# A fused attention and gated-MLP kernel: order of loads and sums around the last 512 rows of the gate stage

## The chip, the cores and the metric

The kernel runs on one core of a Trainium2 chip, in one launch. The metric is the device time of a whole execution in microseconds (us), the median of the runs shown. One more execution is recorded by the hardware profiler; it has a time of its own, and the durations below come from it. The engines of the core are PE (TensorE matmuls; PEld are its weight loads), ACT (ScalarE), DVE (VectorE), POOL (GpSimd) and SP (SyncE, which here only issues transfers). Each takes its own instructions strictly in order. The transfers of all queues run on 16 DMA engines.

## The reference

```
xn = layernorm(x)                                  # x: 2048 x 640, bf16
q  = (xn @ wq) as 32 heads of 192                  # wq: 640 x 6144
k, v = the last 512 of 2048 cached rows, 32 heads of 192
s  = concat(softmax(q k^T / sqrt(192)) v) @ wo     # wo: 6144 x 640
h  = sigmoid(xn @ w_gate) * (xn @ w_up)            # 640 x 1536 each
g  = silu(h @ w_down)                              # w_down: 1536 x 640
out = x + s * g
```

## The kernel before, in words

The kernel has a hand-written order: no scheduler moves an instruction. It has three phases.

**Gate stage (the loop at line 475, to about 134 us of the profile).** The 2048 rows are taken in four steps `s` = 0..3 of 512 rows. Each step has twelve blocks `f` of 128 hidden columns. A block is ten matmuls of 128x512 on PE (line 487: five with the gate weights `wg_sb`, five with the up weights `wu_sb`), a sigmoid on ACT (L492) and a product on DVE (L493) that writes `hT_sb`. The two results of a block take one pair of PSUM banks out of four pairs in turn, so block `f+4` can't start before the sigmoid of block `f` has read its first bank, nor its second half before the product of block `f` has read the second.

The rows of step `s+1` are normalized during step `s` (`ln_at`): statistics on DVE, then at block 4 a square root on ACT (L365, with a table load before and after it), then `ln_rest` at blocks 5 and 6: DVE writes the normalized rows `xn` (L372) and SP issues their DMA transpose (L441), two per block. Steps 1 and 3 use the one buffer `x_odd`; steps 0 and 2 use `x_even[0]` and `x_even[1]`, which lie in the tile `mid`.

Into the same loop a hand-made list puts other work, keyed by (step, block):

- `scan_loads`, `scan_act`, `folds`: the weights `wq` are read in 16 pieces to find a magnitude for scaling them. SP loads a piece (L201), ACT sums its absolute values (L300), or DVE folds it into a running maximum `wmax` (L207, L209).
- `abs_at`: ACT sums the absolute values of `w_up` in four parts (L303).
- L523 reduces `wmax`; `set_scale` (L212 to L217) reduces all sums, rounds to a power of two and has SP issue a small DMA transpose `mx_row`; `set_scale2` (L220 to L222) takes the maximum over the partitions and sets `w_up` (the scale by which `wq` is multiplied; a column of `w_sc`) and `w_down` (that of the keys).
- `swap` at the start of steps 1 and 3: four SP transfers (L445 to L448) that exchange halves of the partitions of `x_even` and `x_odd` into `XC` and `x_sw`. `sums` says at which blocks DVE does the six sums `sum_x` of a pair of steps (L455 to L465, 64x2560 each) that read them. The query projection in the next phase is done with such sums (a Strassen-like scheme).
- In step 3: `scale_w` at blocks 0, 2, 5, 8 (ACT, one L244 and two L249) and `sum_w` at blocks 1, 3, 6, 9 (DVE L262, L263, L265, L266, with one ACT copy L249 between) prepare the query weights, and POOL issues the load of the next piece (L230). `scale_k` (DVE L167) at blocks 0 and 7 and `turn_k` (SP DMA transpose L172) at blocks 3 and 9 prepare the first two key tiles; their raw keys come by `load_k` (L158).

The results `hT_sb` of steps 0 to 2 are written to DRAM (`h_d`, L548). Step 3 uses its own at once: four output tiles `q`, each of twelve pairs of matmuls, 128x512 and 128x128 (L557), with the down weights `wd_sb`, then sigmoid and product (L564, L565).

**Attention (lines 763 to 966, about 134 to 660 us).** Sixteen runs of scores (L697), exponentials (L701), values (L711) and query products (L603).

**End (from line 1109).** The output products and the rest of the gate products (L1019), then the output.

SP's queue around the change stands in this order: scan pieces and `h_d` of step 1, three raw pieces of `wq` (L230); in step 2 two transposes of `x_odd`, `mx_row`, two more transposes, `wd_sb` (L528), four `v_sb` (L181), two `kraw` (L158), four `h_d`; in step 3 `swap`, then the key transposes. SP has eight completion semaphores that it uses in turn, so that a transfer is not issued before the eighth one ahead of it has landed.

Of the kernel before, what the change touches and what calls it, by code (L numbers as in the profile page):

```python
# [17 lines left out]
def kernel(  # L18
# [13 lines left out]
    nc = tc.nc  # L32
# [17 lines left out]
    TQ = 4  # L50
# [28 lines left out]
    def bank2():  # L79
        if bank_order:  # L80
            b = bank_order.pop(0)
        else:
            b = ring.pop(0)
            ring.append(b)
        return ps_all[:, 2 * b:2 * b + 2, :]
# [9 lines left out]
    h_d = [dram.tile([P, NF, P], BF16, name=f"h_d{t}") for t in range(NM3 * TQ)]  # L95
# [58 lines left out]
    def load_k(key, eng=nc.sync):  # L154
        kraw = kraw_pool.tile([P, 2, KC * PC, HF], BF16, name="kraw")
        for i in range(2):
            hk = (2 * (key[0] * G + key[1]) + i) // rep
            eng.dma_start(  # L158
                kraw[:, i, :, :],
                A_k_cache[0, hk, Sk - W:Sk, :].rearrange("(p k) (j e) -> p (k j) e", k=KC, e=HF),  # L160
            )
        kraw_of[key] = kraw
# [56 lines left out]
    def set_scale2(mx=mx, up=w_up, down=w_down, k=1.0 / 4096):  # L219
        nc.vector.tensor_reduce(mx, mx_row[:, 0, :], axis=mybir.AxisListType.X, op=ALU.max)  # L220
        nc.vector.tensor_scalar(down, mx, k, None, op0=ALU.mult)
        nc.vector.reciprocal(up, down)  # L222
# [3 lines left out]
    def load_raw(g, c, eng):  # L226
        raw = raws[raw_next[0] % 3]
        raw_next[0] += 1
        for r in (LO, HI):
            eng.dma_start(raw[r], wq_r[:, c, :, g * GC:(g + 1) * GC])  # L230
        raw_t[g, c] = raw
# [43 lines left out]
    with ExitStack() as bctx:  # L275
# [167 lines left out]
        def swap(pi):  # L443
            x_sw = xt_pool.tile([P, 2, NCD, 512], BF16, name="x_sw")
            nc.sync.dma_start(XC[pi][LO], x_odd[HI])  # L445
            nc.sync.dma_start(XC[pi][HI], x_odd[HI])
            nc.sync.dma_start(x_sw[HI, 0], x_even[pi][LO])
            nc.sync.dma_start(x_sw[HI, 1], x_odd[LO])  # L448
            return x_sw

        def sum_x(pi, k, x_sw):
# [12 lines left out]
            elif k == 5:  # L464
                tt(xb[HI], ev[HI], xb[HI], ALU.subtract)  # L465

        sums = {(1, 4): (0, 4), (1, 10): (0, 0), (1, 11): (0, 1), (2, 7): (0, 2), (2, 8): (0, 3), (2, 10): (0, 5),
                (3, 4): (1, 0), (3, 5): (1, 1), (3, 8): (1, 2)}
        folds = {(1, 7): 9, (1, 8): 10, (1, 9): 11}
        scan_act = {(0, 7): 0, (0, 8): 1, (0, 9): 2, (0, 10): 3, (1, 1): 4, (1, 2): 5, (1, 3): 6, (1, 5): 7, (1, 6): 8,  # L470
                    (2, 0): 12, (2, 1): 13, (2, 2): 14, (2, 3): 15}
        scan_loads = {(0, 8): (4, 5, 6), (0, 9): (7,), (0, 10): (8,), (0, 11): (9,), (1, 1): (10, 11), (1, 7): (12, 13, 14, 15)}
        abs_at = [(0, 3), (0, 4), (2, 6), (2, 8)]
        ln_at = {0: (2, (1, 1, 2), 5), 1: (0, (1, 1, 1, 1), 4), 2: (0, (1, 1, 1, 1), 4)}
        for s in range(NST):
            hT_sb = hpool.tile([P, TQ, NF, P], BF16, name="hT_sb")
            pi = s // 2
            if s % 2 == 1:
                sw = swap(pi)
            for f in range(NF):  # L480
                if s == 0 and f < FA:
                    gu = gu_first[f]
                else:
                    gu = bank2()
                    for i, w in enumerate((wg_sb, wu_sb)):
                        for c in range(NCD):
                            nc.tensor.matmul(  # L487
                                gu[:, i, :], lhsT=w[:, c, f * P:(f + 1) * P], rhs=xnT[s][:, c, :],
                                start=(c == 0), stop=(c == NCD - 1),
                            )  # L490
                sig_sb = bwork.tile([P, 512], BF16, name="sig_sb")
                nc.scalar.activation(sig_sb[:], gu[:, 0, :], AF.Sigmoid)  # L492
                nc.vector.tensor_tensor(  # L493
                    hT_sb[:, :, f, :], *(v.rearrange("p (q n) -> p q n", q=TQ) for v in (gu[:, 1, :], sig_sb[:])),
                    ALU.mult,
                )
                if s + 1 < NST:
                    t = (s + 1) * TQ
                    f0, counts, f1 = ln_at[s]
                    n = f - f0  # L500
                    if 0 <= n < len(counts):
                        for q in range(sum(counts[:n]), sum(counts[:n + 1])):
                            ln_stats(t + q)
                    if f == f1:
                        ln_rstd(t, t + TQ)
                    n = f - f1 - (1 if s else 0)
                    if 0 <= n < 2:
                        ln_rest(t + 2 * n)
                        ln_rest(t + 2 * n + 1)
                if (s, f) in sums:  # L510
                    sum_x(*sums[s, f], sw)
                if (s, f) in folds:
                    scan_fold(wmax, folds[s, f], folds[s, f] == 9)
                if (s, f) in scan_act:
                    scan_abs(scan_act[s, f], 1 + list(scan_act).index((s, f)))
                if (s, f) in abs_at:
                    abs_up(abs_at.index((s, f)))
                if (s, f) in ((0, 8), (1, 7)):
                    load_x4(s + 2)
                for i in scan_loads.get((s, f), ()):  # L520
                    scan_load(i, nc.sync)
                if s == 2 and f == 4:
                    nc.vector.tensor_reduce(  # L523
                        scans[:, 0:1], wmax[:].rearrange("p c n -> p (c n)"), axis=mybir.AxisListType.X, op=ALU.max)
                elif s == 2 and f == 5:
                    set_scale(scans[:])
                elif s == 2 and f == 8:
                    nc.sync.dma_start(wd_sb[:], B_w_down.rearrange("(f p) d -> p f d", p=P))  # L528
                    for hp in range(G):
                        load_v(0, hp, nc.sync)  # L530
                    load_k((0, 0), nc.sync)
                elif s == 2 and f == 9:
                    set_scale2()
                if s == 3:
                    for c in {0: (0,), 2: (1,), 5: (2,), 8: (3,)}.get(f, ()):
                        scale_w(0, c)
                    for c in {1: (0,), 3: (1,), 6: (2,), 9: (3,)}.get(f, ()):
                        sum_w(0, c)
                        load_raw((c + 3) // NCD, (c + 3) % NCD, nc.gpsimd)
                    if f in (0, 7):  # L540
                        scale_k((0, f // 7))
                    elif f in (3, 9):
                        turn_k((0, f // 9))
                    if f == 0:
                        load_k((0, 1), nc.gpsimd)
            if s < NM3:
                for q in range(TQ):
                    nc.sync.dma_start(h_d[s * TQ + q][:], hT_sb[:, q, :, :])  # L548
                if s == 1:
                    for c in range(3):  # L550
                        load_raw(0, c, nc.sync)
                continue
            for q in range(TQ):
                oB_ps = flat(bank2())
                for f in range(NF):
                    for d0, dsz in d_chunks:
                        nc.tensor.matmul(  # L557
                            oB_ps[:, d0:d0 + dsz], lhsT=hT_sb[:, q, f, :],
                            rhs=wd_sb[:, f, d0:d0 + dsz],
                            start=(f == 0), stop=(f == NF - 1),  # L560
                        )
                gB_sb = gpool.tile([P, D], BF16, name="gB_sb")
                sg = bone.tile([P, D], F32, name="sg")
                nc.scalar.activation(sg[:], oB_ps[:, 0:D], AF.Sigmoid)  # L564
                nc.vector.tensor_tensor(gB_sb[:], oB_ps[:, 0:D], sg[:], ALU.mult)  # L565
                if q == 0:
                    scale_w(0, NCD - 1)
                elif q < 3:
                    scale_raw(1, q - 1)
                if q == 1:  # L570
                    sum_w(0, NCD - 1)
                    load_raw(1, 2, nc.gpsimd)
                if q < 3:
                    sum_x(pi, 3 + q, sw)
                else:
                    load_k((1, 0), nc.gpsimd)
                t = s * TQ + q
                nc.gpsimd.dma_start(gB_d[t * P:(t + 1) * P, :], gB_sb[:])
# [633 lines left out]
```

## Time and profile before

| | us |
|---|---|
| median of 3 runs | 881.51 (880.75 to 882.6) |
| the profiled execution: its own time | 882.16 |
| its span | 880.3 |
| PE busy | 866.7 (98%) |
| DVE busy | 674.6 (77%) |
| ACT busy | 625.5 (71%) |
| POOL busy | 212.1 (24%) |
| granted PE clock | 1.00 of full speed |

In the rows of the profile, an arrow points from what is read to what is written, `x5` counts instructions that were merged, and a bracket at the end of a timeline row is the time for which the engine was idle before it and what ended that. Ends of matmuls are modelled and reach about 0.16 us into the next row, so intervals are taken from start to start.

### The profile page before, as it was taken

To read this page: it belongs to the slowest core of one execution; us is meant where nothing else is said; L and a number is where in the kernel's file an instruction comes from. 1 tells how busy PE (TensorE), PEld (TensorE's weight loads), DVE (VectorE), ACT (ScalarE), POOL (GpSimd) and SP (SyncE) were. 2 spreads that over 40 slices of the span, in tenths; PEclk is the share of its full clock that TensorE was granted. 3 is DMA by queue.
4 is the path that set the end of the run, shared out by engine and by line. 5 is a ranking of instruction groups with operands and counts; after the bars stand their busy time and mean duration, and the time that the engine had idled before them with its cause. 6 is when DMAs were issued, how large, how long until landed. Compare 5 with 4: busy or idle time off the path is not lost.

```text
span 880.3 us, 18970 instructions
## 1 busy us (share of the span) xinstructions
PE 866.7 (98%) x7558; PEld 567.4 (64%) x7569; DVE 674.6 (77%) x1137; ACT 625.5 (71%) x772; POOL 212.1 (24%) x299
## 2 busy tenths in 40 slices
PE   9999989999999999999999999999999999999998
PEld 5444445757657757757757757757677777777776
DVE  6587477777777777777777777787978687989997
ACT  6858566578978978878878788684655667666662
POOL 0000118607227227217317316300000111000000
PEclk9999999999999999999999999999999999999999
DMA  9998953298698798699798789598688798565851
GB/s 268 267 273 198 306 102 96 73 235 149 179 253 146 179 257 144 186 242 162 174 229 144 185 182 165 145 290 215 179 223 225 227 299 266 161 222 207 277 168 38
DMA packets 264712, 174.69 MB, mean 198 GB/s; under 512 B 162256, under 2 KB 249680, under 8 KB 264624
## 3 DMA queue, kind: packets, MB, share of 16 engines
q1 hardware_dynamic: 258192, 153.23, 67.7%
q0 software_dynamic: 6432, 20.26, 11.5%
q8 instruction: 59, 0.97, 0.5%
q14 instruction: 29, 0.24, 0.1%
HBM read 102.11 MB, written 35.13 MB: 156 GB/s over the span
## 4 chain that ended last, share of the span: by engine, by line
PE 88%; ACT 4%; DVE 2%; DMA 2%; issue 2%; SPq 2%; ACTq 0%; DVEq 0%
PE ps_all L1019 24%; PE ps_all L603 20%; PE ps_all L711 20%; PE ps_all L697 19%; PE ps_all L487 2%; ACT mid L300 1%; DMA x_sw<-x_odd 1%; PE ps_all L557 1%; ACT sig_sb L492 1%; DVE hT_sb L493 1%; SPq L181 1%; DMA mid<-in_A_wq_dram 1%; PE ps_all L395 1%; DMA x_sb<-in_A_x_dram 0%; ACT L492 0%
## 5 line engine op out<-in xcount | busy, mean ns | idle before, releaser
L701 ACT ACTIVATE E<-ps_all 128x1024 bf16<-128x1024 f32 x256 | 251.1, 1022 | 113.5 <-PE ps_all L697 112.9
L697 PE MATMUL ps_all<-qT,kT 64*128 64x512 bf16 x1536 | 198.1, 376 | 0.0
L711 PEld LDWEIGHTS <-E 128*128 128x128 bf16 x2048 | 169.7, 98 | 8.1 <-issue 8.1
L711 PE MATMUL ps_all<-v_sb,E 128*128 128x193 bf16 x2048 | 174.0, 247 | 0.0
L641 DVE TENSOR_TENSOR qT<-ps_all,qp 128x512 bf16<-128x512 f32 x174 | 115.5, 687 | 48.4 <-PE ps_all L603 36.8
L1019 PEld LDWEIGHTS <-mid 128*128 128x128 f16 x1176 | 115.0, 98 | 44.6
L697 PEld LDWEIGHTS <-kT 64*128 64x128 bf16 x1536 | 85.0, 94 | 79.4 <-issue 4.4
L624 DVE COPY qp<-ps_all 128x512 f32<-128x512 f32 x150 | 100.5, 686 | 45.7 <-PE ps_all L603 45.7
L718 DVE TENSOR_TENSOR o_st<-ps_all,rden 128x768 bf16<-128x768 f32 x128 | 122.5, 957 | 4.4
L603 PE MATMUL ps_all<-mid 64*128 64x512 f16 (+1 forms) x840 | 106.2, 376 | 0.4 <-DVE qT L641 0.4
L603 PE MATMUL ps_all<-mid,arm 64*128 64x512 f16 (+1 forms) x840 | 105.6, 376 | 0.0
L603 PEld LDWEIGHTS <-mid 64*128 64x128 f16 x840 | 49.1, 94 | 43.7 <-issue 1.4
L603 PEld LDWEIGHTS <-arm 64*128 64x128 f16 x840 | 47.1, 94 | 44.5
L1019 PE MATMUL ps_all<-arm,mid 128*128 128x320 f16 x462 | 67.5, 299 | 0.0
L832 ACT ACTIVATE mid<-mid,w_sc 128x1536 f16<-128x1536 bf16 (+1 forms) x41 | 60.2, 1493 | 0.5 <-DMA mid<-oT_d 0.5
L244 ACT ACTIVATE mid<-mid,w_sc 128x1536 f16<-128x1536 bf16 x37 | 58.2, 1572 | 0.6
L1019 PE MATMUL ps_all<-op,mid 128*128 128x320 f16 x378 | 55.1, 299 | 0.0
L493 DVE TENSOR_TENSOR hT_sb<-ps_all,sig_sb 128x512 bf16<-128x512 f32 x48 | 32.7, 685 | 25.0 <-ACT sig_sb L492 15.9
L230 POOL DMA_DIRECT2D mid<-in_A_wq_dram x74 | 43.9, 598 | 21.8 <-DVE mid L266 21.8
L1019 PE MATMUL ps_all<-mid 128*128 128x320 f16 x336 | 48.2, 299 | 0.0
L262 POOL TENSOR_TENSOR arm<-mid 128x384 f16<-128x384 f16 x20 | 18.1, 904 | 114.7 <-ACT mid L244 113.6
L717 DVE RECIPROCAL rden<-ps_all 128x4 f32<-128x4 f32 x128 | 23.3, 182 | 28.4 <-PE ps_all L711 27.0
(185 smaller groups left out, 1058.0 us busy)
## 6 DMA issues: line engine op xcount, KB each, us to landing
oT_d<-oT SPq DMA_DIRECT2D x64, 384.0 KB, 5.6
mid<-oT_d SPq DMA_DIRECT2D x46, 384.0 KB, 4.7
mid<-in_A_wq_dram POOLq DMA_DIRECT2D x74, 192.0 KB, 6.3
mid<-in_A_wq_dram SPq DMA_DIRECT2D x16, 480.0 KB, 7.7
arm<-in_A_wo_dram SPq DMA_DIRECT2D x16, 480.0 KB, 5.4
v_sb<-in_A_v_cache_dram SPq DMA_DIRECT2D x32, 192.0 KB, 6.0
kraw<-in_A_k_cache_dram SPq DMA_DIRECT2D x28, 192.0 KB, 3.7
h_d<-hT_sb SPq DMA_DIRECT2D x12, 384.0 KB, 7.0
```

The source lines that it names most:

```text
L230: eng.dma_start(raw[r], wq_r[:, c, :, g * GC:(g + 1) * GC])
L244: nc.scalar.activation(raw.bitcast(F16), raw, AF.Copy, scale=w_up)
L493: nc.vector.tensor_tensor(hT_sb[:, :, f, :], *(v.rearrange("p (q n) -> p q n", q=TQ) for v in (gu[:, 1, :], sig_sb[:])), ALU.mult,)
L603: nc.tensor.matmul(ps_all[:, b, :], lhsT=w(r, c), rhs=x[r, c, :], start=(first and k == 0), stop=(k == len(cs) - 1), skip_group_check=True,)
L624: nc.vector.tensor_copy(dst, part(b))
L641: nc.vector.tensor_tensor(q_out(i, u, pp), part(b), t, ALU.add)
L697: nc.tensor.matmul(ps[:, b, :], lhsT=kT[h, c * PC + j, :], rhs=qT_t[r][i, j][h, pp, :], start=(j == 0), stop=(j == PC - 1),)
L701: nc.scalar.activation(E_t[r, i, pp][:, c, :, :], ps, AF.Exp, scale=scale_qk)
L711: nc.tensor.matmul(o_ps[:, q // 2, q % 2, 0:DH + 1], lhsT=E[:, c, h, q * P:(q + 1) * P], rhs=vt[:, c, 0:DH + 1], start=(c == 0), stop=(c = ...
L718: nc.vector.tensor_tensor(o_st[:, :, h * DH:(h + 1) * DH].rearrange("p (b i) d -> p b i d", b=2), o_ps[:, :, :, 0:DH], rden[:].to_broadcas ...
L832: eng.activation(t, t.bitcast(BF16), AF.Copy, scale=up)
L1019: nc.tensor.matmul(ps_all[:, b, d0:d1], lhsT=a[:, c, :], rhs=w[:, c, d0:d1], start=(start and c == 0), stop=(c == nk - 1), skip_group_chec ...
```

## The change

All of it lies in the gate stage. The list of work is the same, instruction for instruction; its order on DVE, ACT and SP differs.

- The loads of the first keys (`load_k((0, 0))`) go from step 2, block 8, behind the down weights and values, to the end of step 1, behind the raw `wq` pieces.
- `wd_sb` goes from step 2, block 8, to step 3, block 1. The values go to step 3, block 5.
- The `h_d` stores of step 2 go from the end of step 2 to step 3, block 1, ahead of `wd_sb`. So `swap` is what SP issues first in step 3.
- The reduction of `wmax` and `set_scale` go from step 2, blocks 4 and 5, to block 8; `set_scale2` from block 9 to block 11. So `mx_row` stands behind all four transposes of `x_odd`.
- Scan pieces 14 and 15: ACT takes them at step 2, blocks 5 and 7, behind the square root, in place of blocks 2 and 3 ahead of it; they are loaded two blocks later, and pieces 7 and 8, whose buffers they take, are summed one block later in step 1. The last two parts of `w_up` go from blocks 6 and 8 to 9 and 10.
- Of the sums, one goes a block back in step 2 (8 to 9), and three in step 3 from blocks 4, 5, 8 to 2, 4, 7.

```diff
-        sums = {(1, 4): (0, 4), (1, 10): (0, 0), (1, 11): (0, 1), (2, 7): (0, 2), (2, 8): (0, 3), (2, 10): (0, 5),
-                (3, 4): (1, 0), (3, 5): (1, 1), (3, 8): (1, 2)}
+        sums = {(1, 4): (0, 4), (1, 10): (0, 0), (1, 11): (0, 1), (2, 7): (0, 2), (2, 9): (0, 3), (2, 10): (0, 5),
+                (3, 2): (1, 0), (3, 4): (1, 1), (3, 7): (1, 2)}
         folds = {(1, 7): 9, (1, 8): 10, (1, 9): 11}
-        scan_act = {(0, 7): 0, (0, 8): 1, (0, 9): 2, (0, 10): 3, (1, 1): 4, (1, 2): 5, (1, 3): 6, (1, 5): 7, (1, 6): 8,
-                    (2, 0): 12, (2, 1): 13, (2, 2): 14, (2, 3): 15}
-        scan_loads = {(0, 8): (4, 5, 6), (0, 9): (7,), (0, 10): (8,), (0, 11): (9,), (1, 1): (10, 11), (1, 7): (12, 13, 14, 15)}
-        abs_at = [(0, 3), (0, 4), (2, 6), (2, 8)]
+        scan_act = {(0, 7): 0, (0, 8): 1, (0, 9): 2, (0, 10): 3, (1, 1): 4, (1, 2): 5, (1, 3): 6, (1, 6): 7, (1, 7): 8,
+                    (2, 0): 12, (2, 1): 13, (2, 5): 14, (2, 7): 15}
+        scan_loads = {(0, 8): (4, 5, 6), (0, 9): (7,), (0, 10): (8,), (0, 11): (9,), (1, 1): (10, 11), (1, 7): (12, 13), (1, 9): (14, 15)}
+        abs_at = [(0, 3), (0, 4), (2, 9), (2, 10)]
...
-                if s == 2 and f == 4:
+                if s == 2 and f == 8:
                     nc.vector.tensor_reduce(
                         scans[:, 0:1], wmax[:].rearrange("p c n -> p (c n)"), axis=mybir.AxisListType.X, op=ALU.max)
-                elif s == 2 and f == 5:
                     set_scale(scans[:])
-                elif s == 2 and f == 8:
+                elif s == 2 and f == 11:
+                    set_scale2()
+                elif s == 3 and f == 1:
+                    for q in range(TQ):
+                        nc.sync.dma_start(h_d[2 * TQ + q][:], h_last[:, q, :, :])
                     nc.sync.dma_start(wd_sb[:], B_w_down.rearrange("(f p) d -> p f d", p=P))
+                elif s == 3 and f == 5:
                     for hp in range(G):
                         load_v(0, hp, nc.sync)
-                    load_k((0, 0), nc.sync)
-                elif s == 2 and f == 9:
-                    set_scale2()
...
             if s < NM3:
-                for q in range(TQ):
+                h_last = hT_sb
+                for q in range(TQ) if s < 2 else ():
                     nc.sync.dma_start(h_d[s * TQ + q][:], hT_sb[:, q, :, :])
                 if s == 1:
                     for c in range(3):
                         load_raw(0, c, nc.sync)
+                    load_k((0, 0), nc.sync)
                 continue
```

## The prediction

> **What bounds the kernel now.** I read the page first, then the windows by stage, then PE's waits.
>
> ```profile
> span 880.3 us, 18970 instructions
> 75.00:100.00 25.00, 23.75 (x110) 10.69 (x110) 15.75 (x28) 13.49 (x19) 0.17 (x1) 1.00 0.83 203
> 100.00:124.00 24.00, 18.33 (x88) 8.04 (x89) 17.10 (x32) 15.57 (x23) 5.78 (x10) 1.00 0.91 194
> 200.00:660.00 460.00, 460.00 (x4642) 311.21 (x4640) 350.11 (x596) 359.87 (x426) 154.53 (x204) 1.00 0.86 192
> ```
>
> After the window come its length and the busy time of PE, PEld, DVE, ACT, POOL, then the granted clock and the share and rate of the DMA engines. From 200 to 660 us PE never stops: this stretch has one length, and whatever is won or lost ahead of it moves the whole rest. Between 100 and 124 us PE is busy for 18.33 of 24 us. That is step 3 of the gate stage, which the change reorders. The clock is 1.00 throughout, so only idle time can be won.
>
> ```profile
> PE ps_all L487 <- ACT sig_sb L492: 2.4, 4, 1.0
> PE ps_all L557 <- DVE hT_sb L493: 2.2, 2, 2.1
> PE ps_all L487 <- issue: 1.1, 1, 1.1
> PE ps_all L487 <- DVE hT_sb L493: 0.9, 1, 0.9
> ```
>
> These four rows of PE's waits (total, times, longest) sum to 6.6 us. They leave out the 0.16 us by which modelled ends reach into a gap, so I measure the loss from start to start, on PE's timeline:
>
> ```profile
> 61.06 1.24 PE L487 MATMUL ps_all<-mid,wg_sb 128*128 128x512 bf16 x5 [0.23 <-DMA mid<-xn]
> ...
> 85.88 1.24 PE L487 MATMUL ps_all<-mid,wu_sb 128*128 128x512 bf16 x5
> 88.26 1.24 PE L487 MATMUL ps_all<-x_odd,wg_sb 128*128 128x512 bf16 x5 [1.14 <-issue]
> ...
> 102.00 1.24 PE L487 MATMUL ps_all<-x_odd,wg_sb 128*128 128x512 bf16 x5 [0.59 <-ACT sig_sb L492]
> ...
> 118.36 2.88 PE L557 MATMUL ps_all<-wd_sb,hT_sb 128*128 128x512 bf16 x19
> 123.29 0.45 PE L557 MATMUL ps_all<-wd_sb,hT_sb 128*128 128x512 bf16 x2 [2.05 <-DVE hT_sb L493]
> 123.89 10.22 PE L557 MATMUL ps_all<-wd_sb,hT_sb 128*128 128x512 bf16 x73 [0.15 <-DVE hT_sb L493]
> 134.05 4.84 PE L603 MATMUL ps_all<-mid 64*128 64x512 bf16 x41
> ```
>
> Step 2 runs without a gap: from its first half-block (61.06) to its last (85.88) are 23 half-blocks, 24.82 / 23 = 1.079 us each, 2.158 a block. It ends at 86.96, and three losses follow:
> - Step 3 starts at 88.26: **1.30 us** lost, waiting for `x_odd`.
> - Step 3 takes 118.36 - 88.26 = 30.10 us for 12 x 2.158 = 25.90: **4.20 us** lost.
> - L557 takes 134.05 - 118.36 = 15.69 us. The last 37 of its 48 pairs, which don't stop, take 134.05 - 123.89 = 10.16, 0.275 each, so 48 need 13.18: **2.51 us** lost, waiting for the products of blocks 10 and 11.
>
> Together 8.01 us. That is all that this change can win there.
>
> **Why they are lost.** SP's, DVE's and ACT's timelines show it:
>
> ```profile
> 79.38 2.56 SPq L441 DMA_TRANSPOSE x_odd<-xn  x2
> 82.04 2.13 SPq L217 DMA_TRANSPOSE mx_row<-mx_b  x1
> 84.26 2.55 SPq L441 DMA_TRANSPOSE x_odd<-xn  x2
> ...
> 101.71 1.45 SPq L448 DMA_DIRECT2D x_sw<-x_odd  x1
> ```
> ```profile
> 76.24 2.12 DVE L523 TENSOR_REDUCE scans<-wmax 128x1 f32<-128x1920 bf16 x1
> ...
> 80.16 0.23 DVE L216 CAST mx_b<-w_sc 128x128 bf16<-128x128 f32 x1
> ...
> 80.90 0.79 DVE L372 TENSOR_SCALAR xn<-x_sb,mv,rstd 128x640 bf16<-128x640 bf16 x2
> ...
> 86.45 0.27 DVE L220 TENSOR_REDUCE w_sc<-mx_row 128x1 f32<-128x128 bf16 x1
> ...
> 86.94 0.16 DVE L222 RECIPROCAL w_sc<-w_sc 128x1 f32<-128x1 f32 x1
> ...
> 98.63 0.90 DVE L167 TENSOR_SCALAR k_sb<-kraw,w_sc 128x768 bf16<-128x768 bf16 x2 [7.26 <-DMA kraw<-in_A_k_cache_dram]
> ...
> 112.11 1.49 DVE L457 TENSOR_TENSOR mid<-x_odd,x_sw 64x2560 f16<-64x2560 bf16 x1 [1.57 <-DMA x_sw<-x_odd]
> ...
> 122.55 1.29 DVE L493 TENSOR_TENSOR hT_sb<-ps_all,sig_sb 128x512 bf16<-128x512 f32 x2 [0.42 <-ACT sig_sb L492]
> ```
>
> The last two transposes of `x_odd` stand behind `mx_row` on SP; their issue ends at 86.81 and PE starts 1.45 later. Then DVE stands still for 7.26 us, because `scale_k` (block 0) waits for keys that SP issued last, behind the down weights and the values. Everything behind it on DVE, and on ACT through the copy in `sum_w`, is late from then on: PE stops from 102.00 on for banks, and again in L557. At 112.11 DVE waits once more, for `x_sw`, whose swap SP issued behind all that.
>
> **Part 1, `x_odd`: 1.30 us.** With `mx_row` moved behind, the four transposes follow each other. Even if `xn` comes no earlier than now (80.90 + 0.79 = 81.69), two issues of 1.28 end at 84.25, and with 1.45 on top `x_odd` is there at 85.7, ahead of 86.96. The square root now has two scan pieces of ACT ahead of it in place of four, so it is more likely earlier; the margin of 1.3 us doesn't need it. The key loads are put ahead of these transposes on SP, but issue in step 1's tail. If they slow a transpose, the bound is these 1.30 us back. I take 0 left.
>
> **Part 2, the scale.** The reduction goes to block 8. PE ends this block at 61.06 + 9 x 2.158 = 80.48; its product is done on DVE by about 81.6, the reduction (2.12) at 83.7, four small operations of at most 0.23 at 84.5. SP issues `mx_row` then, with nothing ahead of it.
>
> ```profile
> wd_sb<-in_B_w_down_dram SPq DMA_DIRECT2D x1, 1920.0 KB, 8.3
> ...
> x_sw<-x_odd SPq DMA_DIRECT2D x1, 320.0 KB, 10.4
> ...
> mx_row<-mx_b SPq DMA_TRANSPOSE x1, 3.5
> ```
>
> The last column is us from issue to landing: 3.5 gives 88.0. Meanwhile DVE has three products (two take 1.29 in the last row above, so 0.65 each) and two sums (1.49) to do, 4.9 us, until 89.4, so `set_scale2` doesn't wait: it takes 0.65 (86.45 to 87.10 in the rows) and ends at 90.1. This is a new wait, with step 3's products and `scale_k` behind it on DVE, and ACT's first `scale_w` behind them. The landing lies between 3.5 and, as for the worst queued transfer, 10.4: at 10.4 the scale would come at 95.6. I take 3.5, the same transfer on a queue as empty.
>
> **Part 3, step 3: 4.20 us, and L557: 2.51 us.** With the keys loaded a step earlier, DVE's 7.26 us are gone. The swap is issued from 84.5 + 2.13 = 86.6 on; at most 1.45 each, its last is issued by 91.0 and even at 10.4 lands at 101.4; the sum that reads it stands at block 4, which DVE reaches at about 102. What is next late is the chain between ACT and DVE itself. Its pieces, where nothing else held them, are these rows of ACT:
>
> ```profile
> 90.03 1.57 ACT L244 ACTIVATE mid<-mid,w_sc 128x1536 f16<-128x1536 bf16 x1
> ...
> 92.72 0.60 ACT L492 ACTIVATE sig_sb<-ps_all 128x512 bf16<-128x512 f32 x1
> ...
> 101.36 0.60 ACT L492 ACTIVATE sig_sb<-ps_all 128x512 bf16<-128x512 f32 x1
> ...
> 104.68 0.60 ACT L492 ACTIVATE sig_sb<-ps_all 128x512 bf16<-128x512 f32 x1
> ...
> 107.23 1.08 ACT L492 ACTIVATE sig_sb<-ps_all 128x512 bf16<-128x512 f32 x2
> ...
> 111.04 0.60 ACT L492 ACTIVATE sig_sb<-ps_all 128x512 bf16<-128x512 f32 x1
> ...
> 115.56 1.08 ACT L492 ACTIVATE sig_sb<-ps_all 128x512 bf16<-128x512 f32 x2
> ...
> 119.36 0.60 ACT L492 ACTIVATE sig_sb<-ps_all 128x512 bf16<-128x512 f32 x1
> ```
>
> The sigmoids named are those of blocks 1, 2, 3, 4 (with 5), 6, 7 (with 8) and 9. From `scale_w`'s L244 to the sigmoid of block 1: 2.69. Block 1 to 2 (through `sum_w`, as from 3 to 4): 107.23 - 104.68 = 2.55. 2 to 3: 3.32. 3 to 6: 6.36. 6 to 7: 2.55 again. 7 to 9: 3.80. 9 to the end of the last product: 122.55 + 1.29 - 119.36 = 4.48. So from 90.1: 92.8, 95.3, 98.7, 105.0, 107.6, 111.4, and 115.9 for the last product. Now PE, from 86.96 without a stop: a block's first half may start when the sigmoid four blocks before is done. Block 7 starts at 102.07 (sigmoid 3 done by 99.3), block 10 at 108.54 (sigmoid 6 done by 105.6): no stop, with more than 2.7 us in hand. The sums in blocks 2, 4 and 7 (1.49 each) and `scale_k` in block 7 lie on DVE while ACT does a `scale_w` (2.7). L557 starts at 86.96 + 25.90 = 112.86 and wants block 11 after eleven pairs, at 112.86 + 11 x 0.275 = 115.88. The chain has it at 115.9. So this wait shrinks from 2.2 us to about 0.1, with nothing in hand: each us by which the scale or the chain is later costs a us there.
>
> **Part 4, what goes behind.** The four `h_d` stores wait for the product of the last block of step 2 (89.4), then `wd_sb` is issued: by 92.4 for the swap and at most 1.45 for each store, 98.2. At 8.3 it lands at 106.5, 6.4 ahead of L557. The first L557 waits for the whole of it. [...] The values and key transposes are wanted in the attention phase, more than 20 us on, and `h_d` hundreds of us on. Scan pieces 14 and 15 add no work to ACT, only move it, behind a square root that is now early. These edits cost 0, covered by PE's matmuls of steps 2 and 3; uncovered, a late `wd_sb` costs its lateness.
>
> **Sum.** 1.30 + 4.20 + (2.51 - 0.1) = 7.9 us. The profiled execution took 882.16, 0.65 above the median of 881.51; it becomes 874.3, the median 873.6.
>
> **Rivals.**
> - *The chain is later than its pieces say* (0.20). `mx_row` lands late, or sums meet the chain, and part of L557's wait stays. For it: nothing in hand at 115.9, and a new wait at `set_scale2`. Against it: the queue ahead of `mx_row` is empty. Price: 1 to 5.4 us of the 7.9 (5.4 with the landing at 10.4): 874.6 to 879.0.
> - *It doesn't do what it says* (0.03). PE's stops only move: ACT and DVE carry so much in step 3 that without the waits they set the pace. They are busy for 15.57 and 17.10 of 24 us even where they waited, so this needs another 6 us of chain: 880 to 882.
> - *Slower* (0.05): the down weights come late. They stand behind the swap, four stores and, on the DMA engines, POOL's key and weight loads. It decides from where `wd_sb` lands after 112.86 + 7.9 = 120.8, which is 22.6 us after issue at 98.2, against 8.3 in the row; landing at 125 gives 873.6 + 12.1 = 885.7. [...] Were the weights to take the swap's 10.4, they would still land at 108.6.
>
> **How the numbers follow.** The forecast has the rest, 0.72, with 873.0 to 874.6 for itself. With most of the first rival the range is 872.9 to 877.0. This kernel's measurements can tell about 0.2% (1.8 us) from no change. Faster by more are the forecast and nearly all of the first rival: 0.92. Within it, the second: 0.03. Slower: 0.05.
>
> **What would show it.** In the profile after, step 3's first matmul should follow step 2's at 1.08 us, no wait of PE on `sig_sb` should stand in step 3, `scale_k` should wait for nothing, and L603 should start near 126.1 in place of 134.05. A wait of L557 for `hT_sb` above 1 us would show the first rival, a wait for `wd_sb` the last. Should L603 start early and the span not shrink, the reading that the rest only shifts is wrong.

## The result and the profile after

The changed kernel takes 873.95 us (median of 6 runs, 873.36 to 874.75) against 882.07 before (6 runs, 880.75 to 883.52); the ratio is 0.9908, with a 95% interval of 0.9895 to 0.9921. The forecast was 873.6. The profiled execution took 874.75 with a span of 873.0. Behind the change its line numbers are three higher than before: L557 is now L560, L603 is L606, L711 is L714.

PE's timeline of the changed kernel, the rows that answer to those of before:

```profile
60.80 1.24 PE L487 MATMUL ps_all<-mid,wg_sb 128*128 128x512 bf16 x5
...
85.62 1.24 PE L487 MATMUL ps_all<-mid,wu_sb 128*128 128x512 bf16 x5
86.70 1.24 PE L487 MATMUL ps_all<-x_odd,wg_sb 128*128 128x512 bf16 x5
...
111.52 1.24 PE L487 MATMUL ps_all<-x_odd,wu_sb 128*128 128x512 bf16 x5
112.60 13.28 PE L560 MATMUL ps_all<-wd_sb,hT_sb 128*128 128x512 bf16 x94
125.82 4.84 PE L606 MATMUL ps_all<-mid 64*128 64x512 bf16 x41
```

No row has a bracket any more: step 3 follows step 2 at 1.08 us, takes 25.90 us and hands over to L560, which runs through in 13.22. From the start of step 2 to the query products it is 125.82 - 60.80 = 65.02 us, where before it was 134.05 - 61.06 = 72.99: 7.97 us are gone. The reason stands in SP's and DVE's timelines. Before, these transfers stood ahead of the swap:

```profile
86.86 0.57 SPq L528 DMA_DIRECT2D wd_sb<-in_B_w_down_dram  x1
87.49 6.16 SPq L181 DMA_DIRECT2D v_sb<-in_A_v_cache_dram  x4
93.70 1.80 SPq L158 DMA_DIRECT2D kraw<-in_A_k_cache_dram  x2
95.60 2.49 SPq L548 DMA_DIRECT2D h_d<-hT_sb  x4
98.13 0.91 SPq L445 DMA_DIRECT2D mid<-x_odd  x1
```

Behind the change, SP and DVE show:

```profile
76.10 5.22 SPq L441 DMA_TRANSPOSE x_odd<-xn  x4
84.17 1.14 SPq L217 DMA_TRANSPOSE mx_row<-mx_b  x1
85.49 0.53 SPq L445 DMA_DIRECT2D mid<-x_odd  x1
...
87.68 1.59 SPq L448 DMA_DIRECT2D x_sw<-x_odd  x1
89.31 5.62 SPq L530 DMA_DIRECT2D h_d<-hT_sb  x4
94.98 1.46 SPq L531 DMA_DIRECT2D wd_sb<-in_B_w_down_dram  x1
96.53 12.38 SPq L172 DMA_TRANSPOSE kT<-k_sb  x1
108.96 2.74 SPq L181 DMA_DIRECT2D v_sb<-in_A_v_cache_dram  x4
```
```profile
90.45 0.74 DVE L167 TENSOR_SCALAR k_sb<-kraw,w_sc 128x768 bf16<-128x768 bf16 x2
...
102.32 1.49 DVE L457 TENSOR_TENSOR mid<-x_odd,x_sw 64x2560 f16<-64x2560 bf16 x1
...
114.31 1.29 DVE L493 TENSOR_TENSOR hT_sb<-ps_all,sig_sb 128x512 bf16<-128x512 f32 x2 [0.42 <-ACT sig_sb L492]
```

The four transposes follow each other, the swap is issued 12.6 us earlier than before (L445 at 85.49 for 98.13), and neither `scale_k` nor the sum that reads `x_sw` has a wait in a bracket. The last transfer of the swap lands 17.8 us earlier (87.68 + 6.6 = 94.3 for 112.1); 14.0 of them are its earlier issue (87.68 for 101.71), 3.8 the transfer itself. What stands behind the down weights on SP now stands there long: the key transpose for 12.38 us.

Of the 7.97 us the span shows 7.3. PE's waits name most of the rest, and two rows of the DMA issues (KB each, us from issue to landing) show how soon the swap landed and what came close:

```profile
PE ps_all L714 <- DVE qT L644: 0.7, 1, 0.7
PE ps_all L606 <- DVE qT L644: 0.4, 1, 0.4
```
```profile
x_sw<-x_odd SPq DMA_DIRECT2D x1, 320.0 KB, 6.6
wd_sb<-in_B_w_down_dram SPq DMA_DIRECT2D x1, 1920.0 KB, 15.6
```

The 0.7 us lie at 227 us in the attention phase, where DVE waited for a key load; a second profile of this kernel (below) does not have them. The 0.4 us were there before. And the down weights landed at 94.98 + 15.6 = 110.6, only 2.0 us ahead of L560.

### The profile page after: what moved, and what is told of

Its sections match the earlier page's. It is cut to its first block, busy times and chain, and to the rows that moved or that the text cites. A ratio compares the mean times of both kernels' runs of the same rounds, so it can differ in the third digit from the quotient of the medians.

```text
span 873.0 us, 18973 instructions
## 1 busy us (share of the span) xinstructions
PE 865.2 (99%) x7558; PEld 567.2 (65%) x7569; DVE 674.6 (77%) x1137; ACT 625.4 (72%) x772; POOL 212.1 (24%) x299
## 4 chain that ended last, share of the span: by engine, by line
PE 95%; ACT 1%; DMA 1%; DVE 1%; SPq 1%; issue 0%; ACTq 0%; DVEq 0%
PE ps_all L1022 24%; PE ps_all L714 20%; PE ps_all L606 19%; PE ps_all L700 18%; PE ps_all L487 11%; PE ps_all L560 1%; DMA kraw<-in_A_k_cache_dram 1%; ACT E L704 1%; PE ps_all L395 1%; DMA x_sb<-in_A_x_dram 1%; ACT arm L759 0%; SPq L158 0%; DVE arm L1006 0%; DVE arm L1077 0%; SPq L330 0%
## 5 line engine op out<-in xcount | busy, mean ns | idle before, releaser
L714 PEld LDWEIGHTS <-E 128*128 128x128 bf16 x2048 | 169.7, 98 | 8.9 <-issue 8.9
L714 PE MATMUL ps_all<-v_sb,E 128*128 128x193 bf16 x2048 | 174.1, 247 | 0.7 <-DVE qT L644 0.7
L606 PE MATMUL ps_all<-mid 64*128 64x512 f16 (+1 forms) x840 | 106.2, 376 | 0.4 <-DVE qT L644 0.4
L606 PE MATMUL ps_all<-mid,arm 64*128 64x512 f16 (+1 forms) x840 | 105.6, 376 | 0.0
L606 PEld LDWEIGHTS <-mid 64*128 64x128 f16 x840 | 49.0, 94 | 43.8 <-issue 1.8
L606 PEld LDWEIGHTS <-arm 64*128 64x128 f16 x840 | 47.1, 94 | 44.6 <-issue 0.2
```

The source lines that it names most:

```text
L606: nc.tensor.matmul(ps_all[:, b, :], lhsT=w(r, c), rhs=x[r, c, :], start=(first and k == 0), stop=(k == len(cs) - 1), skip_group_check=True,)
L714: nc.tensor.matmul(o_ps[:, q // 2, q % 2, 0:DH + 1], lhsT=E[:, c, h, q * P:(q + 1) * P], rhs=vt[:, c, 0:DH + 1], start=(c == 0), stop=(c = ...
```

## The experiments

The question was which part of the change carried the 8 us, and how much was left in hand where the prediction said nothing, or much. Each run's ratio is to the kernel before on the same chip.

**1. The first keys alone.** The kernel before, with the key load at the end of step 1:

```diff
@@ step 2, block 8 @@
-                    load_k((0, 0), nc.sync)
@@ end of step 1 @@
                     for c in range(3):
                         load_raw(0, c, nc.sync)
+                    load_k((0, 0), nc.sync)
```

> The kernel before with one edit of the change: the first keys are loaded at the end of step 1. Theory: DVE's stop of 7.26 us for the keys goes, but the next late thing is the swap, which SP still issues behind down weights, values and stores; without the two key loads ahead of it, it is issued only 1.9 us earlier, so x_sw lands at about 110.2 us in place of 112.1, DVE waits there for some 6 us, and L603 starts 1.9 us earlier. So the kernel gains 1.9 us of the 8.1: a time near 880.2, ratio 0.998. Rival (the losses add up, each with its own cause): the stop for the keys carried the lateness of step 3 and L557, 4.2 + 2.5 us, so the gain is 5 to 6.7 us, a time of 875 to 877, ratio 0.992 to 0.994.

Measured: 880.7 us, ratio 0.9986 (0.9976 to 0.9995). DVE's waits, PE's timeline and PE's windows (length, busy PE, PEld, DVE, ACT, POOL, granted clock, DMA share, GB/s):

```profile
DVE mid L455 <- DMA mid<-x_odd: 3.3, 1, 3.3
DVE mid L457 <- DMA x_sw<-x_odd: 3.0, 1, 3.0
```
```profile
120.74 0.45 PE L557 MATMUL ps_all<-wd_sb,hT_sb 128*128 128x512 bf16 x2 [2.06 <-DVE hT_sb L493]
121.33 11.90 PE L557 MATMUL ps_all<-wd_sb,hT_sb 128*128 128x512 bf16 x74 [0.15 <-DVE hT_sb L493]
133.17 1.04 PE L603 MATMUL ps_all<-mid 64*128 64x512 bf16 x8
```
```profile
118.00:121.00 3.00, 0.94 (x8) 0.34 (x6) 2.47 (x7) 1.60 (x3) 1.18 (x2) 1.00 0.40 89
121.00:124.00 3.00, 2.85 (x13) 1.30 (x12) 1.69 (x3) 2.16 (x2) 0.33 (x1) 0.63 0.51 131
```

The 7.26 us for keys are gone, and in their place DVE waits 6.3 us for the swap, as the theory had it; the rival falls. The gain is smaller than its 1.9 us, and the windows show why: after 3 us in which PE was busy for only 0.94, with the stop of 2.06 us in them, the clock granted in the next 3 us was 0.63. The 37 pairs from 121.33 on took 11.84 us in place of 10.16, so 1.7 us of the gain went with the clock.

**2. The change without its swap order.** The changed kernel, with `wd_sb` and the values issued at step 2, block 8, behind `set_scale`, and the stores at the end of step 2:

```diff
                     set_scale(scans[:])
+                    nc.sync.dma_start(wd_sb[:], B_w_down.rearrange("(f p) d -> p f d", p=P))
+                    for hp in range(G):
+                        load_v(0, hp, nc.sync)
...
-                for q in range(TQ) if s < 2 else ():
+                for q in range(TQ):
```

> The changed kernel, but with the down weights, the values and the step-2 stores of h_d where they were, ahead of the swap on SP; keys, scale and sums as changed. Theory: the swap is issued from about 94.7 us on, XC lands near 101 and x_sw near 108.7, the sums at blocks 2 and 4 wait for them on DVE, and the chain to the last product of step 3 ends near 121 in place of 115.6: 5.4 us of the 8.1 are lost again, a time near 879.4, ratio to before 0.997. Rival (the keys were what counted): as the changed kernel, 874, ratio 0.991.

Measured: 880.37 us, ratio 0.9984 (0.9975 to 0.9993), 6.4 us above the changed kernel: most of the 8.1 us are lost again. DVE's waits, PE's timeline and its window:

```profile
DVE mid L455 <- DMA mid<-x_odd: 8.4, 1, 8.4
```
```profile
106.81 2.29 PE L487 MATMUL ps_all<-x_odd,wu_sb 128*128 128x512 bf16 x5 [4.07 <-DVE hT_sb L493]
108.90 1.52 PE L487 MATMUL ps_all<-x_odd,wg_sb 128*128 128x512 bf16 x5
110.26 1.24 PE L487 MATMUL ps_all<-x_odd,wu_sb 128*128 128x512 bf16 x5
```
```profile
106.00:109.00 3.00, 2.19 (x6) 0.79 (x6) 2.47 (x7) 1.52 (x3) 0.64 (x2) 0.51 1.12 178
```

DVE waits 8.4 us at block 2 for `XC`. The theory's 5.4 us are exceeded by 1.0. The clock can account for that: after the stop of 4.07 us it was 0.51, and the ten matmuls from 106.81 to 110.26 took 3.45 us for 2.16, 1.3 us more.

**3. The change without the later scale.** Scan pieces, reduction, `set_scale` and `set_scale2` at their old blocks (and with them the last parts of `w_up` and the sum that went from block 8 to 9 in step 2):

```diff
-                    (2, 0): 12, (2, 1): 13, (2, 5): 14, (2, 7): 15}
+                    (2, 0): 12, (2, 1): 13, (2, 2): 14, (2, 3): 15}
...
-                if s == 2 and f == 8:
+                if s == 2 and f == 4:
                     nc.vector.tensor_reduce(
...
+                elif s == 2 and f == 5:
                     set_scale(scans[:])
-                elif s == 2 and f == 11:
+                elif s == 2 and f == 9:
                     set_scale2()
```

> The changed kernel, but with the scan pieces, the reduction, set_scale and set_scale2 at the blocks they had before, so that mx_row stands between the transposes of x_odd again; keys, swap and sums as changed. Theory: PE waits 1.3 us for x_odd at the start of step 3 and nowhere else, since the chain of ACT and DVE starts at the same time (L244 near 90) and has 1.3 us more in hand: 1.3 us lost, a time near 875.3, ratio 0.9925. Rival (the chain sets the end of step 3 anyway, PE's earlier start is eaten by it): as the changed kernel, 874, ratio 0.991.

Measured: 874.33 us, ratio 0.9915 (0.9899 to 0.9932). PE's timeline:

```profile
86.83 1.24 PE L487 MATMUL ps_all<-x_odd,wg_sb 128*128 128x512 bf16 x5 [0.39 <-DMA x_odd<-xn]
```

The wait for `x_odd` is back, in the place the theory named and nowhere else, but it is 0.39 us (0.56 from start to start), not 1.14. From the start of step 2 (60.37) to the query products (125.86) it takes 65.49 us, 0.47 more than the changed kernel. The time alone can't tell the two readings apart; the profile shows a wait, of less than half of the size.

**4. The scale 2.1 us later.** A second reduction of `wmax` ahead of `set_scale2`:

```diff
                 elif s == 2 and f == 11:
+                    nc.vector.tensor_reduce(
+                        scans[:, 0:1], wmax[:].rearrange("p c n -> p (c n)"), axis=mybir.AxisListType.X, op=ALU.max)
                     set_scale2()
```

> The changed kernel with the reduction of wmax (2.13 us on DVE) done a second time right ahead of set_scale2, so that w_up is set about 2.1 us later. Theory: the chain had nothing in hand (last product of step 3 done at 115.60 where PE wants it at 115.6), so L557 waits for it by 2.1 us: a time near 876.1, ratio 0.993. Rival (the chain takes up delays, since ACT and DVE stand idle for some us in step 3): 0 to 0.5 us, a time of 874 to 874.5, ratio 0.991.

Measured: 875.67 us, ratio 0.9941 (0.992 to 0.9961), 1.7 us above the changed kernel; one of its five runs took 879.98, at a mean clock of 0.998. PE's timeline:

```profile
116.77 0.45 PE L562 MATMUL ps_all<-wd_sb,hT_sb 128*128 128x512 bf16 x2 [1.06 <-DVE hT_sb L493]
```

L562 (L560 of the changed kernel) starts at 112.28 and takes 15.24 us, to 127.52, for 13.22: the 2.1 us come out as 2.0 in the place predicted. The chain of ACT and DVE in step 3 has nothing in hand, though both stand idle for some microseconds in it.

**5. The swap first, alone.** The kernel before with the sums at blocks 2, 4, 7 and only this moved; keys stay at step 2, block 8:

```diff
-                    nc.sync.dma_start(wd_sb[:], B_w_down.rearrange("(f p) d -> p f d", p=P))
-                    for hp in range(G):
-                        load_v(0, hp, nc.sync)
                     load_k((0, 0), nc.sync)
...
+                elif s == 3 and f == 1:
+                    for q in range(TQ):
+                        nc.sync.dma_start(h_d[2 * TQ + q][:], h_last[:, q, :, :])
+                    nc.sync.dma_start(wd_sb[:], B_w_down.rearrange("(f p) d -> p f d", p=P))
+                elif s == 3 and f == 5:
+                    for hp in range(G):
+                        load_v(0, hp, nc.sync)
```

> The kernel before with one part of the change: stores, down weights and values go behind the swap (and the three sums of step 3 to the earlier blocks). The first keys stay at step 2, block 8, where they now stand alone; scale and scan pieces as before. Theory: the order of the swap against the down weights and values is what carries the gain, and the keys are on time wherever nothing large is ahead of them (issued near 85 us, landing near 90, wanted at 89.8). Left is the wait for x_odd, 0.5 us as in the run with the early scale: a time of 874.3 to 875.3, ratio 0.992. Rival (each part has its own share, the keys' early load among them): 1.2 us or more lost to the early load's absence, 876 or later, ratio 0.9935 or above.

Measured: 874.44 us, ratio 0.9919 (0.9905 to 0.9932), against 881.89 before: 7.4 us of gain from one part (stores, down weights and values together). PE's timeline has one gap left in step 3, at the first block, as long as the waits for `x_odd` though the profile names no releaser for it ("issue"):

```profile
87.16 1.24 PE L487 MATMUL ps_all<-x_odd,wg_sb 128*128 128x512 bf16 x5 [0.49 <-issue]
```

So the early load of the keys is not needed. With the down weights and values gone from ahead of them, the keys land 2.6 us after issue from where they always were:

```profile
kraw<-in_A_k_cache_dram SPq DMA_DIRECT2D x2, 192.0 KB, 2.6
```

**6. The sums at their old blocks** (4, 5, 8) in the changed kernel:

```diff
-                (3, 2): (1, 0), (3, 4): (1, 1), (3, 7): (1, 2)}
+                (3, 4): (1, 0), (3, 5): (1, 1), (3, 8): (1, 2)}
```

> The changed kernel with the three sums of step 3 at blocks 4, 5 and 8 as before. Theory: with the swap on time the sums' place matters only through DVE's queue; two sums in neighbouring blocks push the product of block 6 back by 0.6 us and the chain's end by about 0.5, which L557 waits for: a time near 874.5, ratio 0.9915. Rival (the earlier sums are needed for the gain): 2 us or more lost, 876 or later.

Measured: 873.92 us, ratio 0.9913 (0.9899 to 0.9926). PE's timeline:

```profile
115.16 0.45 PE L560 MATMUL ps_all<-wd_sb,hT_sb 128*128 128x512 bf16 x2 [0.22 <-DVE hT_sb L493]
115.76 10.22 PE L560 MATMUL ps_all<-wd_sb,hT_sb 128*128 128x512 bf16 x74 [0.15 <-DVE hT_sb L493]
```

L560 takes 125.92 - 112.07 = 13.85 us for 13.22, 0.6 more, as expected; the time doesn't show it, since single executions scatter by more (those of the changed kernel from 873.36 to 874.75). The rival falls.

**7. The first key transpose later**, at block 9 instead of 3:

```diff
-                    elif f in (3, 9):
-                        turn_k((0, f // 9))
+                    if f == 9:
+                        turn_k((0, 0))
+                        turn_k((0, 1))
```

> The changed kernel with the first key transpose issued at block 9 of step 3 beside the second, in place of block 3. In the profile of the changed kernel the down weights land 15.6 us after issue, at 110.6, 2.0 us ahead of L557, and SP needs 12.4 us for that transpose. Theory: transpose and weights slow each other on the DMA engines, so the weights land near 104 and SP's transposes take 2 to 5 us each; the time stays near 874, since neither is on PE's path. Rival (stores, keys and query weights ahead of the down weights make them late): they land at 109 to 111 as before, same time.

Measured: 873.49 us, ratio 0.9907 (0.9894 to 0.9921). DMA issues and SP's timeline:

```profile
wd_sb<-in_B_w_down_dram SPq DMA_DIRECT2D x1, 1920.0 KB, 16.3
```
```profile
95.72 13.10 SPq L181 DMA_DIRECT2D v_sb<-in_A_v_cache_dram  x4
```

The theory fell: the weights land 16.3 us after issue, at 110.6 as before, and now it is the values that stand on SP for 13.1 us. So the transpose alone doesn't make the weights late. Whether something that stands right behind them does is not shown, since the values took its place there.

**8. The down weights behind the values**, the prediction's slower case made real:

```diff
                 elif s == 3 and f == 1:
...
-                    nc.sync.dma_start(wd_sb[:], B_w_down.rearrange("(f p) d -> p f d", p=P))
                 elif s == 3 and f == 5:
                     for hp in range(G):
                         load_v(0, hp, nc.sync)
+                    nc.sync.dma_start(wd_sb[:], B_w_down.rearrange("(f p) d -> p f d", p=P))
```

> The changed kernel with the down weights issued at step 3, block 5, behind the first key transpose and the four values, in place of block 1. In the profile of the changed kernel they land at 110.6, 2.0 us ahead of L557 (112.6). Theory (the last rival of the prediction, a mechanism with its price): the DMA engines are busy from 86 to 112 us, so what goes ahead adds its own time: values (0.79 MB) and the key transpose (0.39 MB) at some 240 GB/s are 3.3 to 4.9 us, the weights land at 114 to 115.5, and PE waits 1.5 to 3 us for them: a time of 875.5 to 877, ratio 0.993 to 0.9945. Rival: the weights land late only because SP's queue was full of them, and issued alone they land 8 us after issue, before 112.6: as the changed kernel, 874.

Measured: 884.9 us (879.42 to 886.29 in 10 runs), ratio 1.003 (1.0011 to 1.005). Seven runs took 883.9 to 886.3 us at a mean clock of 0.994, three 879.4 to 881.2 at 0.996 to 0.998. The profiled one is the longest, so the sizes below are its own; what the three were spared stays open. PE's timeline, the windows and the DMA issues:

```profile
123.00 15.30 PE L560 MATMUL ps_all<-wd_sb,hT_sb 128*128 128x512 bf16 x96 [10.22 <-DMA wd_sb<-in_B_w_down_dram]
138.24 4.84 PE L606 MATMUL ps_all<-mid 64*128 64x512 bf16 x41
```
```profile
95.00:100.00 5.00, 5.00 (x25) 2.27 (x24) 3.30 (x5) 3.84 (x6) 1.20 (x2) 1.00 1.06 333
100.00:109.00 9.00, 9.00 (x44) 4.05 (x42) 7.04 (x13) 7.01 (x11) 2.34 (x4) 1.00 1.19 125
112.00:123.00 11.00, 0.78 (x4) 0.17 (x3) 3.06 (x7) 1.60 (x3) 1.17 (x2) 0.73 1.12 266
123.00:128.00 5.00, 5.00 (x21) 2.48 (x22) 0.00 (x0) 0.00 (x0) 0.00 (x0) 0.57 0.12 27
```
```profile
wd_sb<-in_B_w_down_dram SPq DMA_DIRECT2D x1, 1920.0 KB, 17.4
```

PE waits 10.2 us for the weights, and then 96 matmuls take 15.24 us for 13.22, because the clock in their first 5 us is 0.57. The rival falls as far as it was made real: issued at 105.5 the weights need 17.4 us and not 8, though they were not alone, with key transpose and values still under way. The theory's direction held and its rate did not: I took 240 GB/s, about the 237 that 1.97 MB in the 8.3 us of before make, and between 100 and 109 us, with the key transpose and the values under way, the DMA engines moved 125 GB/s at a busy share of 1.19. Its forecast of 877 at most was missed for that and for the clock, which it left out.

**9. The changed kernel again, and a better version.** In the changed kernel L606 waits 0.35 us (0.5 from start to start) for the second copy of its first results, which stands behind ACT's table load for the exponential. The load goes ahead of the first copy, where ACT waits anyway. ACT's timeline of the changed kernel:

```profile
127.64 0.60 ACT L625 ACTIVATE qp<-ps_all 128x512 f32<-128x512 f32 x1 [1.02 <-DVE gB_sb L568]
128.26 1.28 ACT L776 ACT_TABLE_LOAD   x1
```

```diff
-        slots[k]()
         if n == 0:
             nc.scalar.activation(mx, w_up, AF.Exp, scale=0.0)
+        slots[k]()
```

> The changed kernel with the small exponential that makes ACT load its table put ahead of the first copy of the query phase instead of behind it, where ACT waits 1.0 us for the last gate product anyway. Theory: the stop of 0.35 us of L606 (0.5 from start to start) goes, so the time is 0.5 us below the changed kernel, 873.4, ratio to before 0.990, and the profile shows no wait of L606 for qT. Rival (the table load has to wait for the same thing, or the copies come no earlier): as the changed kernel, 874, with the same wait.

Measured: 873.01 us, ratio 0.9902 (0.9888 to 0.9915). ACT's and PE's timelines:

```profile
126.38 1.28 ACT L775 ACT_TABLE_LOAD   x1
...
127.78 1.06 ACT L625 ACTIVATE qp<-ps_all 128x512 f32<-128x512 f32 x2
```
```profile
125.55 11.91 PE L606 MATMUL ps_all<-mid 64*128 64x512 bf16 x105
```

The two copies now follow each other and L606 has no bracket. Beside the changed kernel on one chip, and with the late key transpose added:

> The changed kernel as it is, beside the next two on one chip: 873.9, ratio 0.991. Whether the wait of 0.7 us in the value stage near 227 us of its profile (DVE waiting for keys) comes again: by theory it is of one execution and not of the change, so it does not.

> The changed kernel with ACT's table load ahead of the first copy of the query phase, a second time, beside the changed kernel. Theory: 0.5 us (the stop of L606) to 0.9 us (the difference of the medians so far) below it, 873.0 to 873.4. Rival: the difference so far was scatter between chips: the same as the changed kernel within 0.2 us.

> The changed kernel with the table load ahead and the first key transpose at block 9. Theory: the late key transpose moves nothing on PE's path, so it is as the run with the table load alone, 873.0 to 873.4. Rival (the 0.4 us by which the median of the late transpose lay below the changed kernel is real): 872.6 to 873.0.

Measured: the changed kernel 873.53 (873.38 to 873.98), the table load first 873.13 (873.06 to 873.20), both edits 873.01 (872.68 to 873.87); ratios 0.992, 0.9914, 0.9914. The table load is worth 0.4 us (0.5 expected), and its slowest run is below the fastest of the changed kernel; the late transpose adds nothing that can be told. The second profile of the changed kernel has no wait of PE after 140 us, so the 0.7 us at 227 us belonged to one execution.

## Why the prediction was right, and where its working was not

**The sum held, in part by luck.** 7.9 us were forecast up to the query products, 7.97 measured between two profiled executions. The one of before took 882.16 us at a clock of 1.00. The 21 other runs at 0.999 or 1.0 that were made beside the experiments took 879.75 to 881.6, so its losses were larger than is usual at that clock; between the medians the clock fills the difference (below). The chain is closest: sigmoids of blocks 1, 2, 3, 6, 7, 9 were forecast at 92.8, 95.3, 98.7, 105.0, 107.6, 111.4 and started at 92.53, 95.09, 98.41, 104.77, 107.33, 111.13, each 0.2 to 0.3 earlier, as the scale was (89.8 for 90.1) and all of step 2 (60.80 for 61.06). Its end was forecast at 115.9, PE's demand at 115.88; measured are 114.31 + 1.29 = 115.60 and 112.60 + 11 x 0.275 = 115.63. "Nothing in hand" was right to a few hundredths, and the fourth experiment showed that a delay is passed on nearly whole. One wait was left out of the working: the sum at block 2 reads `XC`, and only `x_sw` for block 4 was followed. It came in time, but in the second experiment it is the wait of 8.4 us.

**The cause was put on the wrong transfer.** The prediction told the lateness of step 3 as the keys' 7.26 us, with the swap as a second wait. The first experiment takes the keys' wait away and gains 1.2 us by its ratio; the fifth leaves the keys' load where it was and gains 7.4. What cost the time was what SP had ahead of both: the down weights and the values, and for the swap the stores too. How the loss divides among the three was not tried. The sum came out right because the change moves both, and because the loss was measured on PE and not summed over the waits of DVE.

**`x_odd`, 1.30 us.** The mechanism held, the size seems to be that of one execution. With the same order of transposes the first, third and fifth experiments show PE waiting 0.53, 0.39 and 0.49 us (0.6 to 0.7 from start to start), and up to the last of these transposes the fifth is the kernel before, unaltered. So a usual gain probably has 0.6 to 0.7 us from this term rather than 1.3.

**`wd_sb`, "6.4 us ahead of L557".** This step failed. The 8.3 us to landing were those of a load that was issued at 86.9 onto DMA engines with a busy share of 0.42 in the 2.8 us before; issued behind the swap and the stores, onto engines with a share of 1.01 in the 5 us before, it took 15.6, and 2.0 us were left in hand. From the early place, with the values issued right behind it, it took 8.1 and 8.3 in the first and second experiment too. The 10.4 us of the swap, which the slower rival lent the weights, say nothing of a load behind others or of what the weights do to the swap: the weights had landed at 95.2, before the swap was issued, and the swap of step 1 took 10.4 as well. The late landing changed nothing in the sum, but the slower rival, given 0.05, was nearer than its working said: the eighth experiment reaches it by issuing the weights 10.6 us later.

**"Only idle time can be won."** Also wrong, in about half of the executions. Of 43 runs of the kernel before that were made beside these experiments, 21 have a mean granted clock of 0.999 or 1.0 and a median of 880.6 us, 22 have 0.998 and 882.1. In the first, second and eighth experiment such a loss is seen in place, right behind a stop of PE. The profiled execution of before had 1.00, so its rows couldn't show it. That the dip in those 22 runs follows the stops of 2 us in L557, as in the first experiment, is inferred; they have no trace. The changed kernel's runs are all at 0.999 or 1.0. Beside its second series (873.53) on one chip, the ten runs of before at 0.999 or 1.0 have a median of 880.4, a gain of 6.9 us, and the four at 0.998 one of 881.7, a gain of 8.2. So about 1 us of the 8.1 between the medians seems to be clock, which the prediction counted as nothing; without it the gain is about 1 us under the forecast.

**The rest only shifts.** It did: in the second profile of the changed kernel L606 starts at 125.42, 8.6 us earlier than L603 before, and the span is 8.6 us shorter (871.7 for 880.3).

## What to carry to other kernels

When several waits follow one another on an engine, removing the first can only show the next, as here DVE's 7.26 us for the keys gave way to 6.3 for the swap: ask what all the late transfers have ahead of them in their queue, and move that. Measure the loss on the engine that sets the end, from start to start, and walk the chain of what remains to see how much is in hand; here it was nothing, which no busy share shows. A landing time read where a transfer stood before is no price for it in another place: the down weights took 8.3 us there and 15.6 behind swap and stores.

## What the runs showed of the hardware that was not expected

- The clock granted to PE fell behind two stops and made them dearer than their own length: by 1.3 us for one of 4.07 us (second experiment) and by 2.0 us for one of 10.2 (eighth, 96 matmuls in 15.24 us for 13.22). It was 0.51 for the 3 us with the end of the first and what follows, 0.57 for the 5 us after the second. It also fell in the first experiment, to 0.63, after a stop of only 2.06 us (PE busy for 0.94 of 3 us), and cost 1.7 us; the profile of the kernel before has a stop of 2.05 us in the same place and stays at 1.00. What decides between the two is not shown.
- The 1.97 MB of down weights took 8.1 to 8.3 us on DMA engines that had been busy for 0 to 4 tenths of the 1.9 us just before (three profiles), 13.5 to 17.1 behind swap and stores (eight profiles, issued between 93.98 and 96.50 and landed between 109.8 and 111.6), and 17.4 behind the values. What SP issued next behind swap, stores and weights stood nearly as long: 12.4 us for a key transpose in the changed kernel, 13.1 for the values in the seventh experiment.
- In the eighth experiment, with a key transpose and values under way, DMA engines at a busy share of 1.19 moved 125 GB/s between 100 and 109 us. In the 5 us before it was 333, at a share of 1.06. What lowered the rate is not shown.
